# Moving operands of 512 columns read by turns from their two halves

## The chip, the core and the metric

The kernel runs on one core of a Trainium2 chip. A core has five engines that work beside each other and wait for each other through semaphores: TensorE (PE in the rows, with PEld for the loads of its stationary operand), VectorE (DVE), ScalarE (ACT), GpSimd (POOL) and SyncE (SP), which here issues nearly all DMAs. Matrix products are written by TensorE into eight PSUM banks of 128 partitions x 512 float32; VectorE and ScalarE read them there. Everything else lies in SBUF, 128 partitions wide. The metric is the device time of one execution in microseconds (us); lower is better.

## The reference

What has to be computed is an attention inside chunks of 64 tokens, followed by a gated feed-forward layer on all 4608 tokens, in float32:

```python
# q, k, v: (8, 8, 576, 64), chunks of 64 tokens
scores = scale * np.matmul(q_c, k_c.transpose(0, 1, 2, 4, 3))
scores = scores - np.max(scores, axis=-1, keepdims=True)
attn = np.exp(scores)
attn = attn / (np.sum(attn, axis=-1, keepdims=True) + 1e-09)
out = np.matmul(attn, v_c)
# x: the same numbers as (4608 tokens, 512)
g = x @ w_gate                       # 512 x 1536
silu = g * (1.0 / (1.0 + np.exp(-g)))
val = x @ w_val                      # 512 x 1536
return (silu * val @ w_out)          # 1536 x 512
```

## The kernel before, in words

**Tiling.** The 4608 tokens are nine blocks of 512. The 1536 inner features are twelve groups (`f`) of 128. A product of the feed-forward layer is a chain of matmuls into one PSUM bank, 128 features x 512 tokens. Each factor is kept as two parts of type float32r, an upper one (`hi`, `xh`, `hh`) and the rest (`lo`, `xl`, `hl`), and each product is the sum of three matmuls (lo times hi, hi times lo, hi times hi). The stationary operand is a 128x128 piece of weights (or, in `project`, of activations), loaded anew for each matmul; the moving operand has 512 columns of 4 bytes, side by side in SBUF.

**Stages.** In the opening (`opening`, a written list of steps) the scores, the softmax and the attention of blocks 0 and 1 are done, with the first matmuls of the layer (`some`, line 507) between them. For `f` 2 and 3 whole products follow (`gate`, `value`). From `f` 4 on (`first_seven`) blocks 0 and 1 are taken as a pair, and eight products of quarters are replaced by seven (`seventh`, line 919) whose results are combined by copies on ScalarE (lines 959, 967, 978) and additions on VectorE (`add`, line 923). Then block 2 is done with whole products (line 507), and blocks 3 to 8 in three pairs: twelve `gated_steps` with the seven products of line 919, each followed by some of the output product (`Left.project`, `quarter_of`, line 1283), and then `seven_products`, where the rest of the output product runs in units (`unit`, line 1283). Its results are taken by `snapshot` (ScalarE, line 1386) and `finish` (VectorE, line 1383), turned back by 32x32 transposes and stored. The last three units of the last pair are done for 384 tokens (line 1283) and then for the other 128 with 256 moving columns (`unit_by_tokens`, line 1369).

**Who reads a bank.** ScalarE: the silu of a gate (lines 539, 1005, 1440), the plain copies (959, 967, 978, 1413, 1415, 1417), `snapshot` (1386) and the evacuation of the output tokens of blocks 0 to 2 (line 587, which also swaps columns: `mixed`, `parted`). VectorE: the product with the value (`times`, line 546, where its input is a bank), `add` (923) and `finish` (1383). A bank is refilled when its reader is done; `ps1` is refilled three times in each step.

**Order.** PE, ACT and DVE are under a manual schedule throughout: each engine's instructions run in the order of the program. SP and POOL are scheduled freely after the start.

Other operands that the prediction compares with: line 696 (`B`) subtracts a maximum in PSUM with the moving operand `top[...].broadcast_to(...)`, 512 columns that are 8 numbers of 4 bytes, each read 64 times; lines 94 and 102 (`scale`, `below`) are reads by ScalarE whose neighbouring elements lie 8 bytes apart for `t<-raw`, and, through `order = parted, mixed`, 16 bytes apart for `wo<-raw` and `o_sb<-raw`; line 1574 and the last use of line 1383 (`back`) read a bank as `p (u s) -> p s u`, that is, by turns from two places 512 or 1024 bytes apart.

Of the kernel before, what the change touches and what calls it, by code (L numbers as in the profile page):

```python
# [14 lines left out]
ALU = mybir.AluOpType  # L15
# [18 lines left out]
def attn_then_gated_ffn(ctx: ExitStack, tc: tile.TileContext, qk, v, wgv, wo, out):  # L34
# [25 lines left out]
    def keep_warm_long(n):  # L60

        ps = ps_gv.tile([P, T, P], F32, name="unread", tag="ps_gv")
        for _ in range(n):
            nc.tensor.matmul(ps, ident, ident.rearrange("p (o k) -> p o k", o=1).broadcast_to([P, T, P]), start=True, stop=True)

# [437 lines left out]
    def some(ps, a, f, g, which, first=True, last=True):  # L503
        for k, i in which:
            w = (w_hi, w_lo, w_hi)[i][f][:, g, k]
            x = a.x[k // 2][i == 0][:, k % 2]
            nc.tensor.matmul(ps, w, x, start=first and (k, i) == which[0], stop=last and (k, i) == which[-1])  # L507
# [29 lines left out]
    def silu(pg):  # L537
        h = hp.tile([P, N], F32, name="h")
        nc.scalar.activation(h, pg, AF.Silu, scale=2.0 ** -8)
        return h  # L540
# [4 lines left out]
    def times(h, pv):  # L545
        nc.vector.scalar_tensor_tensor(out=h, in0=pv, scalar=2.0 ** -8, in1=h, op0=ALU.mult, op1=ALU.mult)  # L546

    def gated(a, f):
        h = gate(a, f)
        times(h, value(a, f))  # L550
        return h
# [10 lines left out]
    def project(parts, wo_f, which=range(T)):  # L562
# [6 lines left out]
        for t in which:  # L569
            ts, o = slice(t * P, (t + 1) * P), a.o[t]  # L570
            for at in (slice(0, DM // 2), slice(DM // 2, DM)) if (a.b, f) == (1, 2) or (a.b, f, t < 3) == (1, 3, True) else (slice(0, DM),):
                nc.tensor.matmul(o[:, at], hl[:, ts], woh[:, at], start=f == a.steps[0], stop=False)  # L572
            nc.tensor.matmul(o, hh[:, ts], wol, start=False, stop=False)  # L573
            nc.tensor.matmul(o, hh[:, ts], woh, start=False, stop=f == a.steps[1])  # L574
            if f == a.steps[1]:
# [11 lines left out]
                nc.scalar.activation(mixed(o_sb), parted(o), AF.Copy, scale=2.0 ** -8)  # L587
# [244 lines left out]
    for do in opening.split():  # L832
# [21 lines left out]
        elif do[0] == "Q":  # L854
            b, f = int(do[1]), int(do[2])
            times(rows_of[b, f], products[f"{'VD'[b]}{f}"].ps)
        else:
            b, i = int(do[1]), int(do[2])
            pairs = do[0] in "STCUL"
            getattr(couples[b, i // 2 if pairs else i], do[0])(i if pairs else int(do[3:] or 0))  # L860
# [10 lines left out]
    for f in range(2, SEVEN):  # L871
# [7 lines left out]
        times(h1, pv1)  # L879
# [9 lines left out]
        times(h0, pv0)  # L889
# [20 lines left out]
    times(h1, pv1)  # L910
# [3 lines left out]
    def seventh(ps, x, factors, i, first):  # L914
        which, q = FACTORS[i]
        w = [t.rearrange("p (i k m) -> p i k m", i=4, m=P)[:, q] for t in factors[which]]
        for k in range(NK // 2):
            for n, (u, v) in enumerate(((0, 1), (1, 0), (0, 0))):
                nc.tensor.matmul(ps, w[u][:, k], x[i][v][:, k], start=first and k == 0 and n == 0,  # L919
                                 stop=k == NK // 2 - 1 and n == 2, skip_group_check=True)  # L920

    def add(t, ps):
        nc.vector.tensor_tensor(out=t, in0=t, in1=ps, op=ALU.add)  # L923
# [8 lines left out]
    def first_seven(f, done, before):  # L932
# [26 lines left out]
        nc.scalar.copy(out=h, in_=ps1)  # L959
# [7 lines left out]
        nc.scalar.copy(out=v2, in_=ps2)  # L967
# [10 lines left out]
        nc.scalar.copy(out=v1, in_=ps1)  # L978
# [26 lines left out]
        nc.scalar.activation(h2, ps1, AF.Silu, scale=2.0 ** -8)  # L1005
# [273 lines left out]
    def quarter_of(to, hi, lo, w, u, first, at=slice(0, N), terms=range(3)):  # L1279
        w = w.rearrange("p j (u m) -> p j u m", u=2)  # L1280
        for n in terms:
            a, i = ((lo, 0), (hi, 1), (hi, 0))[n]
            nc.tensor.matmul(to, w[:, i, u], a[:, at], start=first and n == 0, stop=n == 2, skip_group_check=True)  # L1283

    class Seven(Pair):
# [96 lines left out]
        def finish(self, c, ps):  # L1382
            nc.vector.scalar_tensor_tensor(out=c, in0=ps, scalar=2.0 ** -8, in1=c, op0=ALU.mult, op1=ALU.add)

        def snapshot(self, c, ps):
            nc.scalar.activation(c, ps, AF.Copy, scale=2.0 ** -8)
# [13 lines left out]
    def gated_steps(pair, middle, mid, behind, bursts, nothing=lambda: None):  # L1400
        for f in range(NF):
# [11 lines left out]
            nc.scalar.copy(out=h, in_=ps1)  # L1413
            seventh(ps2, pair.x, loaded[f], 1, True)
            nc.scalar.copy(out=v2, in_=ps2)
            seventh(ps1, pair.x, loaded[f], 2, False)
            nc.scalar.copy(out=v1, in_=ps1)
# [22 lines left out]
            nc.scalar.activation(h2, ps1, AF.Silu, scale=2.0 ** -8)  # L1440
# [22 lines left out]
    def seven_products(pair, n):  # L1463
# [117 lines left out]
        pair.finish(back, ps.rearrange("p (u s) -> p s u", u=2))  # L1581
# [153 lines left out]
```

## Time and profile before

| | us |
|---|---|
| median of 3 runs (lowest, highest) | 865.46 (864.99, 865.77) |
| the profiled execution | 864.5 |
| its span, first to last instruction | 862.7 |
| PE busy in it | 853.7 (99%) |
| DVE busy | 652.7 (76%) |
| ACT busy | 424.5 (49%) |
| DMA, mean over the span | 252 GB/s |
| mean granted TensorE clock | 0.999 |

The profiled execution lies 1.0 us under the median, and 1.8 us of it lie outside its span. Read PE's 99% with care: a matmul's recorded duration holds the drain of the array, and the next one starts before it ends, so a row with one duration does not say how often a matmul can start. That is read from the starts of neighbouring rows.

### The profile page before, as it was taken

Reading aid. Unit: us, or ns where it says so; the run is one execution under the profiler, and the core shown is the slowest. Engines: PE = TensorE matmul, PEld = TensorE weight load, DVE = VectorE, ACT = ScalarE, POOL = GpSimd, SP = SyncE. Lnnn points to the kernel's source line nnn. Section 1 sums busy time; section 2 is a strip of 40 time slices with the busy share of each in tenths; the row PEclk is TensorE's granted clock in tenths of the full one; section 3 lists DMA queues with packets and bytes.
Section 4 is the critical chain, followed back from the end, with each engine's and each line's share of the span. In section 5 each row is a group of like instructions: output and inputs, shape, how many; then the busy total and the mean of one; then the engine's idle time right before and its main releaser. Section 6 shows DMA issues by size and latency. Waiting matters only on the chain.

```text
span 862.7 us, 14859 instructions
## 1 busy us (share of the span) xinstructions
PE 853.7 (99%) x5910; PEld 705.4 (82%) x5910; DVE 652.7 (76%) x944; ACT 424.5 (49%) x600; POOL 99.9 (12%) x94
## 2 busy tenths in 40 slices
PE   7999999999999999999999999999999999999998
PEld 5888888888888888888888888888888888888887
DVE  6988999777797673788897985887979943335785
ACT  4957788653524444536435635344346533333362
POOL 2100000000048743433200000000000000000000
PEclk9999999999999999999999999999999999999999
DMA  9967778899998785798976885766756965555562
GB/s 347 336 241 293 265 275 331 321 318 337 299 359 307 269 282 176 263 336 251 300 219 223 262 253 167 280 218 227 206 198 220 281 206 190 188 201 186 189 193 73
DMA packets 126948, 217.50 MB, mean 252 GB/s; under 512 B 56736, under 2 KB 88096, under 8 KB 116896
## 3 DMA queue, kind: packets, MB, share of 16 engines
q1 hardware_dynamic: 124560, 213.68, 72.9%
q10 hardware_dynamic: 2320, 2.88, 1.0%
q8 instruction: 46, 0.75, 0.4%
q14 instruction: 22, 0.18, 0.1%
HBM read 166.72 MB, written 49.81 MB: 251 GB/s over the span
## 4 chain that ended last, share of the span: by engine, by line
PE 97%; DMA 1%; ACT 0%; SPq 0%; issue 0%; DVE 0%; DVEq 0%
PE ps_a L919 28%; PE ps_gv L919 21%; PE ps_o L1283 14%; PE ps_gv L507 13%; PE ps_gv L1283 6%; PE ps_o L572 4%; PE ps_o L573 4%; PE ps_o L574 4%; PE ps_a L313 2%; PE ps_a L398 1%; DMA qk_t<-in_qk 1%; PE ps_a L497 1%; PE ps_a L1369 0%; PE ps_a L483 0%; ACT s_sb L700 0%; ACT pT L723 0%
## 5 line engine op out<-in xcount | busy, mean ns | idle before, releaser
L919 PE MATMUL ps_a<-x,factors 128*128 128x512 f32 x864 | 215.6, 390 | 0.0
L919 PEld LDWEIGHTS ps_a<-x,factors 128*128 128x128 f32 x864 | 161.9, 188 | 34.5 <-ACT s_sb L321 1.0
L919 PE MATMUL ps_gv<-x,factors 128*128 128x512 f32 x648 | 164.5, 389 | 0.0
L919 PEld LDWEIGHTS ps_gv<-x,factors 128*128 128x128 f32 x648 | 121.5, 188 | 25.4
L507 PE MATMUL ps_gv<-xh,w 128*128 128x512 f32 x320 | 97.3, 391 | 0.0
L385 DVE STREAM_TRANSPOSE turned<-s_sb 32x256 f32<-32x256 f32 x192 | 83.6, 436 | 2.7
L1283 PE MATMUL ps_o<-halves,sums 128*128 128x512 f32 (+1 forms) x324 | 72.8, 383 | 0.0
L507 PEld LDWEIGHTS ps_gv<-xh,w 128*128 128x128 f32 x320 | 59.9, 188 | 12.4
L1283 PEld LDWEIGHTS ps_o<-halves,sums 128*128 128x128 f32 x324 | 60.4, 188 | 11.3
L507 PE MATMUL ps_gv<-xl,w 128*128 128x512 f32 x160 | 60.7, 393 | 0.0
L546 DVE SCALAR_TENSOR_TENSOR rows<-v,rows 128x512 f32<-128x512 f32 x72 | 50.6, 703 | 13.2 <-ACT rows L1440 6.0
L923 DVE TENSOR_TENSOR rows<-rows,ps_gv 128x512 f32<-128x512 f32 x36 | 24.6, 685 | 44.5 <-PE ps_gv L919 43.8
L1429 ACT ACTIVATE rows<-rows 128x512 f32<-128x512 f32 x36 | 22.8, 633 | 71.6 <-DVE rows L923 71.6
L1283 PE MATMUL ps_o<-hh,left 128*128 128x512 f32 x216 | 57.7, 394 | 0.0
L1265 ACT CAST hh<-rows 128x512 fp32r<-128x512 f32 x36 | 22.4, 621 | 70.4 <-DVE rows L546 70.4
L572 PE MATMUL ps_o<-both,hh 128*128 128x512 f32 (+1 forms) x151 | 56.4, 381 | 0.0
L573 PE MATMUL ps_o<-both,hh 128*128 128x512 f32 x144 | 56.1, 390 | 0.0
L574 PE MATMUL ps_o<-both,hh 128*128 128x512 f32 x144 | 56.1, 390 | 0.0
L923 DVE TENSOR_TENSOR v<-v,ps_a 128x512 f32<-128x512 f32 x44 | 30.1, 685 | 28.9 <-PE ps_a L919 18.0
L1326 DVE TENSOR_TENSOR halves<-rows,halves 128x1024 fp32r<-128x1024 f32 x36 | 43.2, 1215 | 11.1 <-ACT halves L1322 11.0
L1283 PE MATMUL ps_gv<-halves,sums 128*128 128x512 f32 x216 | 50.4, 389 | 0.0
L1322 ACT CAST halves<-rows 128x1024 fp32r<-128x1024 f32 x36 | 37.2, 1053 | 21.5 <-DVE rows L1300 7.7
(171 smaller groups left out, 1367.0 us busy)
## 6 DMA issues: line engine op xcount, KB each, us to landing
factors<-t SPq DMA_DIRECT2D x36, 1024.0 KB, 6.9
factors<-w SPq DMA_DIRECT2D x36, 512.0 KB, 4.1
w<-w SPq DMA_DIRECT2D x16, 1024.0 KB, 7.8
sums<-s SPq DMA_DIRECT2D x15, 1024.0 KB, 4.9
qk_t<-in_qk SPq DMA_DIRECT2D x26, 512.0 KB, 7.8
t<-th SPq DMA_DIRECT2D x24, 512.0 KB, 3.9
raw<-in_wgv SPq DMA_DIRECT2D x11, 1024.0 KB, 7.7
both<-o SPq DMA_DIRECT2D x22, 512.0 KB, 6.4
```

The lines of the kernel that those rows point to most:

```text
L385: nc.vector.transpose(out=self.turned[to:to + 32, p:p + 2, j, :, 32 * (i % 2):32 * (i % 2) + 32], in_=src[32 * i:32 * i + 32, :, o // 2, 3 ...
L507: nc.tensor.matmul(ps, w, x, start=first and (k, i) == which[0], stop=last and (k, i) == which[-1])
L546: nc.vector.scalar_tensor_tensor(out=h, in0=pv, scalar=2.0 ** -8, in1=h, op0=ALU.mult, op1=ALU.mult)
L572: nc.tensor.matmul(o[:, at], hl[:, ts], woh[:, at], start=f == a.steps[0], stop=False)
L573: nc.tensor.matmul(o, hh[:, ts], wol, start=False, stop=False)
L574: nc.tensor.matmul(o, hh[:, ts], woh, start=False, stop=f == a.steps[1])
L919: nc.tensor.matmul(ps, w[u][:, k], x[i][v][:, k], start=first and k == 0 and n == 0, stop=k == NK // 2 - 1 and n == 2, skip_group_check=True)
L923: nc.vector.tensor_tensor(out=t, in0=t, in1=ps, op=ALU.add)
L1283: nc.tensor.matmul(to, w[:, i, u], a[:, at], start=first and n == 0, stop=n == 2, skip_group_check=True)
L1322: nc.scalar.copy(out=t[:, 0], in_=src)
L1326: nc.vector.tensor_tensor(out=lo, in0=src, in1=hi.bitcast(F32), op=ALU.subtract)
L1429: nc.scalar.activation(h, h, AF.Silu, scale=2.0 ** -8)
```

## The change

Two things are done, always together.

1. The moving operand of the matmuls with 512 columns (and of those with 384, and of the pieces of 256 at line 572) is read through `by_turns`: column 0, column 256, column 1, column 257, and so on. The first index steps by 4 bytes, the inner one jumps by half of the operand (1024 bytes). The columns of the result stand in the bank in that order, without gaps.
2. Whatever reads such a bank reads it through `put_back`: first every second column from 0 on, then every second from 1 on (a step of 8 bytes), and so writes the columns to SBUF in their old order. At line 587 the bank's new order and the swap of columns cancel in part: the bank is read with steps and the output is written side by side.

Not touched: the matmuls of the attention (64x64), the transposes, line 696, and line 1369.

```diff
+    def by_turns(x):
+        return x.rearrange("p (a b) -> p b a", a=2)
+
+    def put_back(ps):
+        return ps.rearrange("p (b a) -> p a b", a=2)
+
+    def in_halves(x):
+        return x.rearrange("p (a b) -> p a b", a=2)
...
-            nc.tensor.matmul(ps, w, x, start=first and (k, i) == which[0], stop=last and (k, i) == which[-1])
+            nc.tensor.matmul(ps, w, by_turns(x), start=first and (k, i) == which[0], stop=last and (k, i) == which[-1])
...
-        nc.scalar.activation(h, pg, AF.Silu, scale=2.0 ** -8)
+        nc.scalar.activation(in_halves(h), put_back(pg), AF.Silu, scale=2.0 ** -8)
...
-    def times(h, pv):
-        nc.vector.scalar_tensor_tensor(out=h, in0=pv, scalar=2.0 ** -8, in1=h, op0=ALU.mult, op1=ALU.mult)
+    def times(h, v):
+        nc.vector.scalar_tensor_tensor(out=h, in0=v, scalar=2.0 ** -8, in1=h, op0=ALU.mult, op1=ALU.mult)
+
+    def times_bank(h, pv):
+        times(in_halves(h), put_back(pv))
...
-                nc.tensor.matmul(o[:, at], hl[:, ts], woh[:, at], start=f == a.steps[0], stop=False)
-            nc.tensor.matmul(o, hh[:, ts], wol, start=False, stop=False)
-            nc.tensor.matmul(o, hh[:, ts], woh, start=False, stop=f == a.steps[1])
+                nc.tensor.matmul(o[:, at], hl[:, ts], by_turns(woh)[:, at.start // 2:at.stop // 2], start=f == a.steps[0], stop=False)
+            nc.tensor.matmul(o, hh[:, ts], by_turns(wol), start=False, stop=False)
+            nc.tensor.matmul(o, hh[:, ts], by_turns(woh), start=False, stop=f == a.steps[1])
...
-                nc.scalar.activation(mixed(o_sb), parted(o), AF.Copy, scale=2.0 ** -8)
+                nc.scalar.activation(o_sb.rearrange("p (h s u) -> p h s u", h=2, u=2), o.rearrange("p (u s h) -> p h s u", h=2, u=2), AF.Copy, scale=2.0 ** -8)
...
-                nc.tensor.matmul(ps, w[u][:, k], x[i][v][:, k], start=first and k == 0 and n == 0,
+                nc.tensor.matmul(ps, w[u][:, k], by_turns(x[i][v][:, k]), start=first and k == 0 and n == 0,
...
     def add(t, ps):
-        nc.vector.tensor_tensor(out=t, in0=t, in1=ps, op=ALU.add)
+        t = in_halves(t)
+        nc.vector.tensor_tensor(out=t, in0=t, in1=put_back(ps), op=ALU.add)
...
-            nc.tensor.matmul(to, w[:, i, u], a[:, at], start=first and n == 0, stop=n == 2, skip_group_check=True)
+            nc.tensor.matmul(to, w[:, i, u], by_turns(a[:, at]), start=first and n == 0, stop=n == 2, skip_group_check=True)
...
         def finish(self, c, ps):
-            nc.vector.scalar_tensor_tensor(out=c, in0=ps, scalar=2.0 ** -8, in1=c, op0=ALU.mult, op1=ALU.add)
+            c = in_halves(c)
+            nc.vector.scalar_tensor_tensor(out=c, in0=put_back(ps), scalar=2.0 ** -8, in1=c, op0=ALU.mult, op1=ALU.add)
 
         def snapshot(self, c, ps):
-            nc.scalar.activation(c, ps, AF.Copy, scale=2.0 ** -8)
+            nc.scalar.activation(in_halves(c), put_back(ps), AF.Copy, scale=2.0 ** -8)
```

The plain copies out of a bank (lines 959, 967, 978, 1413, 1415, 1417) and the silus of lines 1005 and 1440 change as `silu` does; the last `finish` (`back`) is written out as it was, since line 1369 is untouched.

No instruction is added, removed or moved: on every engine the same instructions stand in the same order, on the same buffers. What differs beside the access patterns is some waits: 97 matmuls in place of 27 also wait for an earlier matmul, the nearest of them 15 matmuls back, and 32 additions on VectorE lose a wait for ScalarE.

## Rows read from the trace of the kernel before

**Rows 1.** The page: busy time (share of the span) and instructions; the chain by engine.
```profile
PE 853.7 (99%) x5910; PEld 705.4 (82%) x5910; DVE 652.7 (76%) x944; ACT 424.5 (49%) x600; POOL 99.9 (12%) x94
...
PE 97%; DMA 1%; ACT 0%; SPq 0%; issue 0%; DVE 0%; DVEq 0%
```

**Rows 2.** Whole span, lines 919, 1283, 507, 572, 573 (574 alike): PE (count), PEld.
```profile
0.00:863.00 863.00, 432.22 (x1848) 346.24 (x1848) 1.00 0.74 252
...
0.00:863.00 863.00, 178.51 (x756) 140.82 (x756) 1.00 0.74 252
...
0.00:863.00 863.00, 113.17 (x480) 89.50 (x480) 1.00 0.74 252
...
0.00:863.00 863.00, 56.36 (x151) 28.35 (x151) 1.00 0.74 252
...
0.00:863.00 863.00, 56.09 (x144) 27.04 (x144) 1.00 0.74 252
```

**Rows 3.** Timeline of PE: first start, us to the last end, line, tile, shape, count.
```profile
9.27 0.81 PE L696 MATMUL ps_a<-tops,minus 128*128 128x512 f32 x3
...
619.26 2.88 PE L919 MATMUL ps_a<-x,factors 128*128 128x512 f32 x12
621.98 1.52 PE L919 MATMUL ps_gv<-x,factors 128*128 128x512 f32 x6
...
854.88 1.55 PE L1283 MATMUL ps_o<-halves,sums 128*128 128x384 f32 x8
...
856.61 2.31 PE L1369 MATMUL ps_a<-sums,halves 128*128 128x256 f32 x18
```

**Rows 4.** Lines 696, 919, 1283, 1369: duration in ns, least/median/most.
```profile
L696 PEld LDWEIGHTS ps_a<-tops,minus x16: 186/189/192, 8.9 to 18.8; 128*128 128x128 f32 x16
L696 PE MATMUL ps_a<-tops,minus x16: 379/379/483, 8.9 to 19.0; 128*128 128x512 f32 x16
...
L919 PEld LDWEIGHTS ps_gv<-x,factors x648: 186/188/188, 323.7 to 812.9; 128*128 128x128 f32 x162
...
L919 PEldq EVENT_SEMAPHORE  x31: 51/51/51, 318.5 to 769.9; - x31
...
L1283 PE MATMUL ps_o<-halves,sums x42: 333/334/423, 848.7 to 856.4; 128*128 128x384 f32 x36, 128*128 128x512 f32 x6
...
L1369 PE MATMUL ps_a<-sums,halves x18: 278/283/283, 856.6 to 858.6; 128*128 128x256 f32 x18
```

**Rows 5.** Groups on ACT and DVE by shape: busy us, mean ns, idle before.
```profile
L94 ACT ACTIVATE wo<-raw 128x512 f32<-128x512 f32 x12 | 13.5, 1128 | 0.1
...
L1386 ACT ACTIVATE c<-ps_o 128x512 f32<-128x512 f32 x18 | 10.1, 592 | 6.0 <-PE ps_o L1283 4.7 <-DMA factors<-w 1.0
...
L94 ACT ACTIVATE t<-raw 128x512 f32<-128x512 f32 x2 | 1.3, 674 | 3.0 <-DMA raw<-in_wgv 3.0
...
L1574 ACT COPY back<-pt 128x256 f32<-128x256 f32 x1 | 0.4, 372 | 2.8 <-PE pt L1573 2.8
...
L1383 DVE SCALAR_TENSOR_TENSOR c<-ps_o,c 128x384 f32<-128x384 f32 x2 | 1.1, 557 | 2.6 <-PE ps_o L1283 2.6
L1383 DVE SCALAR_TENSOR_TENSOR back<-ps_a,back 128x256 f32<-128x256 f32 x1 | 0.4, 425 | 1.0 <-PE ps_a L1369 1.0
```

**Rows 6.** By stage: us, busy PE PEld DVE ACT POOL (count), clock, DMA, GB/s.
```profile
84.00:165.00 81.00, 81.00 (x356) 66.38 (x355) 74.27 (x108) 64.97 (x87) 0.00 (x0) 1.00 0.77 299
165.00:215.00 50.00, 50.00 (x469) 41.75 (x468) 33.95 (x61) 21.50 (x34) 0.00 (x0) 1.00 0.95 331
...
458.00:500.00 42.00, 42.00 (x187) 34.77 (x186) 40.05 (x42) 25.69 (x31) 0.00 (x0) 1.00 0.77 250
...
640.00:682.00 42.00, 42.00 (x187) 34.80 (x186) 40.94 (x43) 24.84 (x30) 0.00 (x0) 1.00 0.77 242
```

**Rows 7.** Waits of weight loads, 84 to 165 us: total us, times, longest.
```profile
PEld ps_a L919 <- DVE v L923: 0.4, 1, 0.4
PEld ps_a L919 <- ACT v L978: 0.4, 1, 0.4
```

## What the change does to the time: a prediction

> **What bounds the kernel now.** First the page: TensorE is busy for 853.7 of 862.7 us and makes 97% of the chain that ended last [rows 1]. So what a matmul costs decides, and other engines count only where they make TensorE wait. Second, which matmuls: the counts by line [rows 2] are 1848 + 756 + 480 + 151 + 144 + 144 (line 574 as line 573). Of these, 36 of line 1283 have 384 columns [rows 4] and 14 of line 572 have 256, which leaves 3473 with 512. Third, how often one can start, from the starts in the timeline [rows 3]. Line 919 has 12 matmuls between 619.26 and 621.98 us: 2.72 us / 12 = 226.7 ns. With the granted clock at 0.999 of 2.4 GHz, 512 columns alone would be 213.3 ns. Line 1283 with 384 columns: the eighth starts 1.55 us less one duration of 334 ns [rows 4] after the first, so 1.216 / 7 = 173.7 ns, against 160.0 for the columns. Line 1369 with 256: (2.31 - 0.283) / 17 = 119.2 ns, against 106.7. The surplus is 13.4, 13.7 and 12.5 ns: the same for each matmul, however many columns it has. Fourth, one line is different: 696, also 512 columns, with a weight load of the same length (189 against 188 ns, [rows 4]), starts every (0.81 - 0.379) / 2 = 215.5 ns [rows 3, 4]. Its moving operand is 8 numbers read over and over. Array, weight load and write to PSUM are the same as elsewhere, so 226.7 - 215.5 = 11.2 ns of each matmul belong to the read of a moving operand that runs through memory. As this does not grow with the columns, I take it for something that happens once per matmul; the weight load (128 columns each time) that is read from the same memory meanwhile is my candidate. That is an inference, and no row shows two reads collide.
>
> **The change part by part.** *The moving read.* What a read by turns from two places costs TensorE stands in no row. The bound below: the whole 11.2 ns goes, as in line 696, since then a column that is held up in one half need not hold up the next, which comes from the other. The bound above: reads that leave a 16-byte stretch of SBUF with each element. ScalarE has such a read at line 94: 128x512 from `raw` with a step of 16 bytes takes 1128 ns, with a step of 8 bytes 674 [rows 5], so 454 ns more for 512 elements. Here a read returns to the same stretch with the next column but one, which that row doesn't do. I take the lower bound, since line 696 is the same engine and the same instruction and line 94 is neither, and keep the upper as the first rival.
>
> The Trainium skill speaks against the change here: "Advanced Engine Details and Errata", section "Memory Cachelines", has SBUF lines of 16 bytes, wants two hits on a line for full speed and puts a penalty on a different line with each access. The step of 16 bytes in line 94 agrees with it (1128 against 674 ns). By that rule the sum below would change its sign; whether TensorE keeps two lines at hand no row shows.
>
> The sum: 3473 matmuls with 512 columns and 36 with 384, 3509 x 11.2 ns = 39.3 us, if TensorE never waits more than now. The 14 pieces of 256 I leave at nothing.
>
> *What is late next.* Three places cannot follow. From 84 to 165 us (`first_seven`) TensorE has 356 matmuls, 4.0 us of the sum; weight loads there already wait for the copy at line 978 and the addition at line 923 (0.4 us each, [rows 7]), with VectorE busy for 74.27 and ScalarE for 64.97 of 81 us [rows 6]. `ps1` comes free only when a reader in the middle of their queues is done, and that does not get faster: I keep 1.0 of the 4.0 us. In the two stages of `seven_products` (458 to 500 and 640 to 682 us) TensorE has 187 matmuls, 2.1 us each, and VectorE is busy for 40.05 and 40.94 of 42 us [rows 6]; 42 - 2.1 = 39.9 is less than that. I keep half, 2.1 of 4.2. From 165 to 215 us the DMA engines have a share of 0.95 [rows 6]; I take off 1 us. The opening's first matmuls of line 507, before the softmax chain ends, give nothing: under 0.2 us. Together 39.3 - 3.0 - 2.1 - 1.0 - 0.2 = 33 us. The whole 39.3 stays if all slack suffices; 26.7 if these losses, 6.3 us together, are twice as large.
>
> *The readers of the banks.* They now step by 8 bytes in PSUM. The nearest rows read a bank by turns from two places: ScalarE at line 1574 takes 372 ns for 256 elements, against 592 for 512 side by side at line 1386, that is 0.86 ns for each of the 256 more; VectorE's `back` at line 1383 takes 425 for 256, against 557 for 384 side by side [rows 5], 1.03 ns for each. With a penalty on steps the shorter reads would lie high, and they do not. So I cost the readers at nothing; a gain has no reason, as the elements stay as many; above, 454 ns for each read as in line 94, which is the second rival. They run beside TensorE, except at the places just named.
>
> *The waits.* 70 more matmuls also wait for an earlier matmul, 15 or more before it, so over 3 us back at 215 ns each. Behind them the next matmuls would be held up, and the readers of the banks after them, but what they wait for is long done. What stays is a semaphore instruction on TensorE's queue: the 31 at line 919 take 51 ns each [rows 4], beside running matmuls. Nothing.
>
> Sum against the profiled execution: 864.5 - 33 = 831.5 us. The median of the runs lies 1.0 above that execution: **832.5 us**, told as 833.
>
> **The rivals.** *First, slower: each column is a new line.* If TensorE pays for each column what ScalarE pays at line 94, a matmul takes 226.7 + 454 = 681 ns and the kernel 865.5 + 3473 x 0.454 = 2442 us. If a column costs as much as one element of a plain read does on ScalarE, 0.86 ns as above, it is 440 ns, 213 more, and 1605 us. It decides from any start-to-start time over 226.7 ns, since nothing hides a matmul. For it: line 94, the only row with a line per element in SBUF. Against it: contiguous reads here pay a fixed amount, not one per line, and a read by turns stays in each line for four of its columns.
>
> *Second, slower: the put-back costs.* TensorE gains nothing and each reader of a bank takes 454 ns more. From 84 to 165 us there are seven steps of `first_seven` with three additions of line 923 each: VectorE 74.27 + 21 x 0.454 = 83.8 of 81 us. In each of the two product stages it has at most 8 such reads (line 1383): 43.7 and 44.6 of 42. That is 2.8 + 1.7 + 2.6 = 7 us, 872; and if in each of the 44 steps of seven products one bank is late by those 454 ns, 20 more, 892. It decides once a reader takes longer than the slack that TensorE leaves it. Against it: lines 1574 and 1383 [rows 5].
>
> *Third: the change doesn't do what it says.* The 11.2 ns belong to every read that runs through memory, whatever its order: 865.5 us. For it: all contiguous operands pay it alike. Against it: so fixed an amount looks like a meeting with the weight load. The Trainium skill's "SBUF — State Buffer", section "Who interferes with whom", gives TensorE two independent read ports, one for the moving operand and one for weights; by that my candidate is wrong and this rival is the outcome, though the rule leaves line 696's 215.5 ns unexplained.
>
> **How the numbers follow.** Forecast, faster: 0.66. First rival 0.18, second 0.09, third 0.07. The forecast's own range: with the whole 39.3 us kept 826, and 823 if the surplus over the bare columns goes as well in part; with 26.7 kept 839; with half of the 11.2 ns gone 849. The range that I give is 823 to 895: it takes in the third rival and the second to its 892, 0.82 in all less the tails, and leaves out the first, for whose prices no bound near the others exists. A difference under 0.2%, 1.7 us, is about what a measurement of this kernel cannot tell from no change. Faster 0.66, within it 0.07, slower 0.27 (first and second rival).
>
> **What would show it.** Right: neighbouring matmuls of line 919 and 1283 start about 216 ns apart, their recorded duration falls from 389 to about 379 ns as in line 696, and waits of TensorE for `v`, `h` and `halves` grow to some 6 us in the three stages. The readers keep their durations (592 ns at line 1386). Wrong: starts 227 ns apart (third rival) or some 430 to 680 (first), or copies of line 1413 and additions of line 923 that take a microsecond and more (second). If the starts fall to 216 and the time falls by less than 20 us, my slack was wrong and not the read.

## The result, and the profile after

The changed kernel takes 844.92 us (median of 4 runs, 843.64 to 845.34), the kernel before 865.23 beside it: a ratio of 0.9763, 95% interval 0.9746 to 0.9780. It is faster, by 20 us. Forecast were 833 us and a range of 823 to 895.

Lines have moved: 919 is now 933, 1283 is 1298, 1383 is 1399, 1386 is 1402, 923 is 938, 94 and 102 are 105 and 113, 959 and 978 are 974 and 993, 1326 is 1341, 1373 is 1388. First the page of the profiled execution (span 843.3 us), as in [rows 1]:

```profile
PE 822.9 (98%) x5910; PEld 707.5 (84%) x5910; DVE 656.0 (78%) x944; ACT 438.1 (52%) x600; POOL 100.7 (12%) x94
...
PE 68%; DVE 16%; DMA 6%; ACT 5%; issue 3%; SPq 1%; DVEq 0%; ACTq 0%
```

TensorE was 97% of the chain and is 68% now: VectorE, loads and ScalarE stand between its pieces. Then the starts, as in [rows 3], and the durations and readers, as in [rows 4, 5] (timeline of PE; groups by shape):

```profile
611.72 1.46 PE L933 MATMUL ps_gv<-x,factors 128*128 128x512 f32 x6
613.01 1.46 PE L933 MATMUL ps_a<-x,factors 128*128 128x512 f32 x6
614.31 1.46 PE L933 MATMUL ps_gv<-x,factors 128*128 128x512 f32 x6
```
```profile
L933 PE MATMUL ps_a<-x,factors 128*128 128x512 f32 x864 | 206.8, 380 | 2.7 <-ACT halves L1337 1.5
L1402 ACT ACTIVATE c<-ps_o 128x512 f32<-128x512 f32 x18 | 10.2, 594 | 4.4 <-PE ps_o L1298 4.2
L938 DVE TENSOR_TENSOR v<-v,ps_gv 128x512 f32<-128x512 f32 x44 | 30.1, 684 | 10.2 <-PE ps_gv L933 10.2
```

Twelve matmuls start in 614.31 - 611.72 = 2.59 us, 216 ns each, where it was 226.7. The readers of the banks, which now step by 8 bytes, take what they took (594 ns against 592). But reads of SBUF that the change doesn't touch became slower, if they step (ScalarE's lines 105 and 113 unpack words with steps of 16 and 8 bytes; VectorE's line 1388 turns a block):

```profile
L113 ACT ACTIVATE o_sb<-raw 128x512 int32<-128x512 uint32 x12 | 18.7, 1555 | 0.0
L105 ACT ACTIVATE wo<-raw 128x512 f32<-128x512 f32 x12 | 18.4, 1530 | 0.5 <-DMA raw<-in_wo 0.5
L105 ACT ACTIVATE t<-raw 128x512 f32<-128x512 f32 x2 | 1.3, 662 | 2.6 <-DMA raw<-in_wgv 2.6
...
L1388 DVE STREAM_TRANSPOSE turned<-c 128x512 f32<-128x512 f32 x22 | 19.0, 862 | 0.8
```

The copies of `wo` rose from 1128 [rows 5] to 1530 ns, the transposes from 714 to 862; the two early pieces of `t` (662, before 674), which run before the first matmul by turns, did not change. What TensorE waited for (weight loads, as in [rows 7]), in `first_seven` (86 to 167 us) and in the second stage of `seven_products` (627.5 to 669.5 us; the first stage has the same two rows with 1.3 us each), and these stages as in [rows 6]:

```profile
PEld ps_a L933 <- ACT h L974: 3.4, 4, 1.1
PEld ps_a L933 <- DVE v L938: 2.5, 4, 0.7
PEld ps_a L933 <- ACT v L993: 1.7, 6, 0.7
```
```profile
PEld ps_o L1298 <- DVE halves L1341: 1.5, 2, 0.9
PEld ps_o L1298 <- PE ps_o L1298: 1.3, 1, 1.3
```
```profile
86.00:167.00 81.00, 77.96 (x350) 64.44 (x349) 73.20 (x106) 71.40 (x84) 0.00 (x0) 1.00 0.74 289
167.00:217.00 50.00, 50.00 (x508) 43.44 (x510) 34.87 (x62) 22.49 (x35) 0.00 (x0) 1.00 0.98 344
449.00:491.00 42.00, 40.57 (x186) 34.71 (x185) 38.60 (x40) 26.12 (x33) 0.00 (x0) 1.00 0.78 253
627.50:669.50 42.00, 40.42 (x184) 34.27 (x184) 39.70 (x41) 25.60 (x31) 0.00 (x0) 1.00 0.72 234
```

The row in which line 1298 waits for itself is VectorE's too: that wait is for a semaphore of TensorE and one of VectorE, and in all eight traces that read by turns there it ends 44 to 46 ns after VectorE's subtraction of line 1341 (here at 490.47 and 490.43 us). Where TensorE never paused before, it now pauses, and ScalarE is busy for 71.40 us in the first stage where it was 64.97.

To see where time was won, the table takes the same matmuls in each kernel: the time from the start of the one that began a stretch before to the start of the one that ended it. "Possible" is the count of changed matmuls with 384 or 512 columns in the stretch times 11.2 ns. "Late", "16 bytes", "mixed" and "GpSimd" are experiments 4, 6, 9 and 10 below, "before + GpSimd" is 12. Each column is one profiled execution.

| stretch before, us | possible | before | after | late | 16 bytes | mixed | GpSimd | before + GpSimd |
|---|---|---|---|---|---|---|---|---|
| 0-46 | 0.94 | 44.81 | 46.86 | 44.90 | 44.14 | 45.64 | 45.91 | 45.83 |
| 46-168 | 5.99 | 121.84 | 122.19 | 121.82 | 119.62 | 119.60 | 122.08 | 121.82 |
| 168-345 | 7.94 | 177.12 | 169.81 | 170.48 | 171.17 | 169.92 | 171.11 | 177.12 |
| 345-441 | 4.40 | 96.03 | 93.16 | 93.77 | 93.30 | 92.85 | 92.66 | 96.03 |
| 441-458 | 0.72 | 16.87 | 17.12 | 17.13 | 19.07 | 17.86 | 17.13 | 16.86 |
| 458-500 | 2.08 | 42.16 | 42.25 | 42.25 | 42.06 | 42.25 | 43.37 | 43.23 |
| 500-620 | 5.57 | 119.98 | 114.64 | 114.64 | 114.64 | 114.64 | 114.66 | 120.03 |
| 620-640 | 0.87 | 20.03 | 21.44 | 21.14 | 22.47 | 22.25 | 21.40 | 20.04 |
| 640-682 | 2.07 | 41.93 | 42.40 | 42.40 | 41.85 | 42.03 | 43.16 | 42.99 |
| 682-end | 8.71 | 176.51 | 168.03 | 168.02 | 168.02 | 168.02 | 168.03 | 176.51 |

In all 39.3 us were possible, 19.4 came, 19.9 are lost: 3.0 in the opening, 6.3 from 46 to 168, 1.5 from 345 to 441, 1.0, 2.2, 2.3 and 2.5 in the four stretches around the stages of seven products, 1.1 in the rest. From 500 to 620 and from 682 on nearly all arrives (13.8 of 14.3). The opening differs by some 1 us between executions without any change there (44.81 and 45.83 in the two columns of before).

### The profile page after: what moved, and what is told of

It reads as the page before. It is cut to its first block, busy times and chain, and to the rows that moved or that the text cites. A ratio compares the mean times of both kernels' runs of the same rounds, so it can differ in the third digit from the quotient of the medians.

```text
span 843.3 us, 14878 instructions
## 1 busy us (share of the span) xinstructions
PE 822.9 (98%) x5910; PEld 707.5 (84%) x5910; DVE 656.0 (78%) x944; ACT 438.1 (52%) x600; POOL 100.7 (12%) x94
## 4 chain that ended last, share of the span: by engine, by line
PE 68%; DVE 16%; DMA 6%; ACT 5%; issue 3%; SPq 1%; DVEq 0%; ACTq 0%
PE ps_a L933 21%; PE ps_gv L933 15%; PE ps_o L1298 10%; PE ps_gv L518 9%; DMA raw<-in_wgv 4%; PE ps_o L586 3%; PE ps_o L587 3%; PE ps_o L588 3%; DVE halves L1341 2%; PE ps_gv L1298 2%; DVE turned L396 2%; PE ps_a L324 2%; DMA w<-w 2%; DVE rows L1315 1%; PE ps_a L409 1%
## 5 line engine op out<-in xcount | busy, mean ns | idle before, releaser
L933 PE MATMUL ps_a<-x,factors 128*128 128x512 f32 x864 | 206.8, 380 | 2.7 <-ACT halves L1337 1.5
L933 PE MATMUL ps_gv<-x,factors 128*128 128x512 f32 x648 | 157.7, 379 | 0.0
L518 PE MATMUL ps_gv<-xh,w 128*128 128x512 f32 x320 | 94.0, 380 | 0.2 <-DVE w L157 0.2
L1298 PE MATMUL ps_o<-halves,sums 128*128 128x512 f32 (+1 forms) x324 | 70.5, 375 | 3.0 <-PE ps_o L1298 1.8
L1298 PE MATMUL ps_o<-hh,left 128*128 128x512 f32 x216 | 55.3, 383 | 0.0
L587 PE MATMUL ps_o<-both,hh 128*128 128x512 f32 x144 | 54.6, 379 | 0.0
L588 PE MATMUL ps_o<-both,hh 128*128 128x512 f32 x144 | 54.6, 379 | 0.0
L1298 PE MATMUL ps_gv<-halves,sums 128*128 128x512 f32 x216 | 48.1, 379 | 0.0
```

The lines of the kernel that those rows point to most:

```text
L518: nc.tensor.matmul(ps, w, by_turns(x), start=first and (k, i) == which[0], stop=last and (k, i) == which[-1])
L587: nc.tensor.matmul(o, hh[:, ts], by_turns(wol), start=False, stop=False)
L588: nc.tensor.matmul(o, hh[:, ts], by_turns(woh), start=False, stop=f == a.steps[1])
L933: nc.tensor.matmul(ps, w[u][:, k], by_turns(x[i][v][:, k]), start=first and k == 0 and n == 0, stop=k == NK // 2 - 1 and n == 2, skip_grou ...
L1298: nc.tensor.matmul(to, w[:, i, u], by_turns(a[:, at]), start=first and n == 0, stop=n == 2, skip_group_check=True)
```

## The experiments

**1. The read by itself.** Bursts of 16 and 28 float32r matmuls whose moving operand of 512 columns is read in different orders, also with fewer weight columns, and beside copies of ScalarE and work of VectorE.

```
"four": x.rearrange("p (a b) -> p b a", a=4)        # four places, 512 bytes apart
"two", "step": every second, every fourth number    # steps of 8 and 16 bytes
"pairs": two columns here, two there                "held": 8 numbers over and over
"half", "quarter": side by side, 64 and 32 columns of weights
```

> Nothing of the reference is computed: bursts of 16 and 28 float32r matmuls over data in SBUF. Theory A (the surplus of 11 ns comes from the moving read meeting the weight load's read in the memory): side by side 226.7 ns, held columns 215.5, by turns 215.7; with 64 and 32 columns of weights the surplus of side by side falls to about a half and a quarter (221, 218). Theory B (the surplus is the moving read's own): 226.7 with 64 and 32 columns of weights as well. Theory A for the slower ScalarE (its reads that leave a 16-byte stretch with each element meet a read by turns): beside turns the copy with a 16-byte step takes about 1500 ns, beside side-by-side matmuls about 1100; with a step of 8 bytes about 750 against 670; side by side 590 to 620 in both. Rival: the slowing in the kernel came from elsewhere (DMA, VectorE); then all copies take the same beside either form.

Timeline of PE: start, us to the last end, count; then ScalarE's groups (each three copies: side by side, steps of 8 and of 16 bytes):

```profile
6.32 15.88 PE L79 MATMUL side<-columns,weights 128*128 128x512 f32 x56 [6.32 <-ACT columns L48]
22.25 3.72 PE L79 MATMUL turns<-columns,weights 128*128 128x512 f32 x16
26.03 4.78 PE L79 MATMUL four<-columns,weights 128*128 128x512 f32 x16
30.86 7.47 PE L79 MATMUL two<-columns,weights 128*128 128x512 f32 x16
38.39 7.62 PE L79 MATMUL step<-columns,weights 128*128 128x512 f32 x16
46.07 5.68 PE L79 MATMUL pairs<-columns,weights 128*128 128x512 f32 x16
...
59.42 3.72 PE L79 MATMUL held<-columns,weights 128*128 128x512 f32 x16
63.20 3.91 PE L79 MATMUL half<-columns,weights 128*64 128x512 f32 x16
67.17 3.89 PE L79 MATMUL quarter<-columns,weights 128*32 128x512 f32 x16
```
```profile
L99 ACT COPY turns<-source 128x512 f32<-128x512 f32 x3 | 2.9, 1039 | 0.0
...
L99 ACT COPY side<-source 128x512 f32<-128x512 f32 x3 | 2.2, 793 | 0.0
L99 ACT COPY two<-source 128x512 f32<-128x512 f32 x3 | 2.2, 787 | 0.0
```

Median start to start: side by side 227 ns, by turns 216, one held operand 216, four places 283, pairs 340, steps of 8 and 16 bytes 451 and 461. With 64 and 32 columns of weights, whose loads take 135 and 108 ns in place of 188, a read side by side still takes 231 and 232. So the surplus does not come from meeting the weight load; it is the read's own, and two places by turns are a case apart: four places already cost 67 ns. The three copies beside turns took 621, 891 and 1605 ns one by one, beside a read side by side 623, 649 and 1107, and beside the other four forms at most 673 and 1146 in the last two. What slows ScalarE is not that TensorE leaves a stretch at each column, which "step" does too; and four places, 512 bytes apart at 283 ns, slow nothing (654 and 1119 ns).

**2 and 3. The two halves of the change.** One kernel reads by turns and takes the banks side by side; the other reads side by side and steps through the banks.

```
 2:  def put_back(ps): return ps.rearrange("p (a b) -> p a b", a=2)
 3:  def by_turns(x):  return x.rearrange("p (b a) -> p b a", a=2)
```

> The moving operands are read by turns, the banks are read side by side, so the columns of the result stand in a wrong order. Theory (all of the change, gain and loss, is in TensorE's read): 845 us as with the whole change, lines 94 and 102 at 1500 to 1560 ns. Rival (the put-back readers slow ScalarE's strided reads or delay TensorE): lines 94 and 102 at 1130, and some 832 to 838 us.

> The moving operands are read side by side as before, the banks are read with steps of 8 bytes, so the columns of the result stand in a wrong order. Theory: 865 us, readers of banks at 0.59 (ScalarE) and 0.68 us (VectorE), lines 94 and 102 at 1130 to 1150 ns. Rival: 867 to 872 us and lines 94 and 102 slower.

```profile
L105 ACT ACTIVATE wo<-raw 128x512 f32<-128x512 f32 x12 | 18.4, 1531 | 0.2 <-DMA raw<-in_wo 0.2
```
```profile
L105 ACT ACTIVATE wo<-raw 128x512 f32<-128x512 f32 x12 | 13.5, 1126 | 0.3 <-DMA raw<-in_wo 0.3
```

Turns alone (first row): 844.77 us, ratio 0.9765 (0.9746 to 0.9783), as the whole change, with the slow copies. Putting back alone (second row): 866.35 us, 1.0013 (1.0004 to 1.0023), 1.1 us slower and at most 2.0, copies as before. Gain and harm both lie in TensorE's read; the readers of the banks are all but free.

**4 and 8. Turns only late, turns only early**, parted at the end of `first_seven`, some 171 us.

```
+    by = {"turns": False}         # 8: True
     _, h2 = first_seven(NF - 1, quarters, None)
+    by["turns"] = True            # 8: False
```

> Everything up to the end of first_seven (blocks 0 and 1, about 171 us) is as before, from block 2 on it is as with the change. Theory (the loss in the first 171 us is ScalarE's lines 94 and 102, slowed by the read by turns): these lines back at 1130 to 1150 ns, the first 171 us as before the change, so 2.2 us less than the whole change: 842.7 us. Rival (the two parts are not independent, the late part loses again what the early part keeps): 844 to 846 us.

> Turns of 1024 bytes as in the change until the end of the first seven-product stage at about 171 us, the order of before from there on: the complement of the kernel with late turns. At 171 us the changed kernel was 2.2 us late on the kernel before. Theory A, the loss up to there is real and is not made good: about 865.4 + 2 = 867, between 866 and 869, with the copies of the output weights at 1530 ns and starts of 216 ns up to 171 us and 227 after. Theory B, what is late there is caught up in later waits: 864.5 to 866.

Late turns: 843.97 us, ratio 0.9752 (0.9731 to 0.9774). Early turns: 867.14 us, 1.0018 (1.0009 to 1.0027). Up to 168 us 619 matmuls became shorter by 6.9 us together, and the program is slower for it: that is the harm on its own. Taking it away gave 1 us of 845, within the spread of the runs: of the 2.3 us that "late" was ahead at 168 us (0-46 and 46-168 of the table), it gave 1.3 back by 441.

**5. How far apart the two places lie.** The same bursts with groups in which the places are 8, 16, 64 and 256 bytes apart, halves 1024 apart, and halves moved to 1040.

```
def within(b): return lambda x: x.rearrange("p (g a b) -> p g b a", a=2, b=b)   # b = 2, 4, 16, 64
far = const.tile([P, 2, 260], F32R, name="apart")                               # 1040 bytes
```

> Nothing of the reference is computed here: the kernel holds only bursts of 28 float32r matmuls of 512 columns with other work beside them. The two places that TensorE reads by turns lie 8, 16, 64, 256, 1024 or 1040 bytes apart. Beside each form ScalarE copies 128x512 numbers with a step of 4, 8 and 16 bytes, and VectorE makes a transpose and two sums, one with a step of 16 bytes in one input. In the run of forms the reads in halves (1024 bytes apart) took 216 ns and the stepped copies beside them 891 and 1605 ns, where beside a read side by side they took 649 and 1107; the transpose took 872 and 702, the stepped sum 1532 and 1054. Theory A, the other engines are slowed because TensorE leaves one stretch of memory for another at every column: at 16 bytes' distance it mostly stays in the same stretch, so starts come 216 ns apart there as before while the stepped copies stay near 650 and 1110 ns, the transpose near 700 and the stepped sum near 1060; from some distance on, 64 bytes or more, they rise to about 890, 1600, 870 and 1530. Theory B, what slows them is that TensorE reads without the pauses that the 227 ns of a read side by side contain: then every form with starts 216 ns apart, however near its places are, shows about 890, 1600, 870 and 1530 ns. Theory C, the slowing comes from two places in the same bank, that is from a distance that is a multiple of some power of two: then 1040 bytes would leave the copies near 650 and 1110 ns and 1024 would not.

Start to start: 227 ns at 8 bytes, 216 at 16, 64, 256, 1024 and 1040. VectorE's groups beside them (the number in a name is the distance, "turns" is 1024 and "apart" 1040 bytes; "sumstep" reads one input with a step of 16 bytes, "back" is a transpose):

```profile
L106 DVE TENSOR_TENSOR turnssumstep<-source 128x512 f32<-128x512 f32 x1 | 1.5, 1519 | 0.0
L106 DVE TENSOR_TENSOR by256sumstep<-source 128x512 f32<-128x512 f32 x1 | 1.5, 1517 | 0.0
...
L106 DVE TENSOR_TENSOR apartsumstep<-source 128x512 f32<-128x512 f32 x1 | 1.1, 1096 | 0.0
...
L106 DVE TENSOR_TENSOR by16sumstep<-source 128x512 f32<-128x512 f32 x1 | 1.1, 1057 | 0.0
L106 DVE TENSOR_TENSOR sidesumstep<-source 128x512 f32<-128x512 f32 x1 | 1.1, 1052 | 0.0
...
L101 DVE STREAM_TRANSPOSE turnsback<-source 128x512 f32<-128x512 f32 x1 | 0.9, 870 | 0.0
L101 DVE STREAM_TRANSPOSE by256back<-source 128x512 f32<-128x512 f32 x1 | 0.9, 852 | 0.0
...
L101 DVE STREAM_TRANSPOSE apartback<-source 128x512 f32<-128x512 f32 x1 | 0.7, 705 | 0.0
```

ScalarE's copy with a step of 16 bytes took 1561 and 1605 ns beside 256 and 1024, 1092 to 1131 beside 8, 16, 64 and 1040. Theories A and B fall (64 is free, and so are 16 and 1040 with full speed); C stands as far as it was tried: the others' stepped reads are slowed where the two places lie 256 or 1024 bytes apart, and 16 bytes more than 1024 free them. Why is not shown, and other distances were not tried.

**6 and 7. The whole kernel with 16 and with 64 bytes.** VectorE's scalar_tensor_tensor has at most two steps besides the partition in all these traces, ScalarE's activation three; a bank whose order needs more is read in two instructions here.

```
-        return x.rearrange("p (a b) -> p b a", a=2)
+        return x.rearrange("p (g a b) -> p g b a", a=2, b=4)      # 7: b=16
-        times(in_halves(h), put_back(pv))
+        for i in range(2):
+            times(in_halves(h)[:, :, i], put_back(pv)[:, :, i])
```

> The whole kernel, with the two places that TensorE reads by turns 16 bytes apart instead of 1024 (groups of 8 columns, read 0, 4, 1, 5, 2, 6, 3, 7); the readers of the banks put that order back, in two instructions where VectorE's scalar_tensor_tensor and ScalarE's copy to the output take no more than two steps. Theory A, the loss of the changed kernel (some 19 of 38 us of shorter matmuls) comes largely from ScalarE's and VectorE's stepped reads, slowed because both places lie at a multiple of 256 bytes: starts stay at 216 ns, the copies of the output weights fall from 1530 to about 1130 ns, the turned products of VectorE from 862 to about 715, the gain at 171 us rises from -2.2 to between +1 and +5, and the time falls from 844.9 to between 834 and 842. Theory B, the loss is only TensorE being fast enough to wait for results that come no later than before: the copies fall as well, but the time stays at 843 to 847. Theory C, the extra split of the banks' readers (two instructions of 256 columns for one of 512 at some 50 places, about 0.1 us each) and a third step in the others' addresses cost more than they save: 847 to 853.

> As the kernel before it, with the two places 64 bytes apart (groups of 32 columns). In the run of distances this was as free as 16 bytes: starts 216 ns, transposes 702, stepped sums 1074 for 1057. Theory A: within 1 us of the kernel with 16 bytes, 834 to 842; Theory B: 843 to 847; if the inner runs of 4 columns cost the banks' readers something at 16 bytes, runs of 16 columns cost less, and this kernel is faster than the other by over 1 us.

With 16 bytes: 845.76 us (842.98 to 849.33), ratio 0.9779 (0.9752 to 0.9806); with 64: 845.93, 0.9775 (0.9759 to 0.9792). The slowing is gone while starts stay at 216 ns: copies of `wo` take 1134 ns, and VectorE's transposes with 16 bytes what they took before:

```profile
L1393 DVE STREAM_TRANSPOSE turned<-c 128x512 f32<-128x512 f32 x22 | 15.7, 713 | 0.8
```

And the stretch from 46 to 168 us takes 119.62 instead of 122.19 us (119.65 with 64 bytes), so 2.6 us of the lost 6.3 were this. But the time is the same: theory A is right for that stretch, theory B for the whole. The split has a price: two halves of a sum with a bank take 0.80 us where the whole took 0.67. What was won is lost at 262 to 300, 441 to 458 and 620 to 640 us, by 1.4, 1.9 and 1.0 us.

**9. 16 bytes early, 1024 late**, to tell whether the split readers take that back.

```
+    B, by = 4, {"groups": True}
     _, h2 = first_seven(NF - 1, quarters, None)
+    by["groups"] = False
```

> Places 16 bytes apart until the end of the first seven-product stage (some 171 us), 1024 bytes from there on, with one instruction for each reader of a bank there. The kernel with 16 bytes throughout got the early stretch back (168 us of the program took 165.3 there, 171.1 in the changed kernel) but lost about 1.4, 1.9 and 1.1 us at the three later places (262 to 300, 441 to 458 and 620 to 640 us), which are laid to its split readers. Theory A (that price is the split readers'): the three later stretches go back to 36.6, 17.1 and 21.4 us, the early one stays at 165 to 166, and the time is 839 to 842 us. Theory B (those gaps come from the earlier start of the rest, whatever the readers): they stay, and the time is 844 to 847.

843.93 us (841.78 to 847.70), ratio 0.9759 (0.9735 to 0.9782); the profiled execution has 840.5 us of span. 46 to 168 us stay at 119.60, 262 to 300 go back to 36.64, 441 to 458 to 17.86, but 620 to 640 take 22.25. Half an answer: experiments 2 and 10, whose readers are not split, have 37.81 and 37.98 in the second stretch, so these places move by 1 to 2 us without them.

At two of them the traces point to something that no experiment was made for. TensorE (first rows: experiment 6) stops with no releaser that the profile shows, there in the middle of 128 like matmuls; the last row is a DMA queue of the changed kernel's page (packets, MB, share), of the kind "instruction":

```profile
615.86 2.08 PE L411 MATMUL ps_a<-turned,v_t 64*64 64x64 f32 x120
620.54 0.34 PE L411 MATMUL ps_a<-turned,v_t 64*64 64x64 f32 x8 [2.60 <-issue]
...
q8 instruction: 47, 0.77, 0.4%
```

A packet of 16 KB of that queue landed at 619.17 us, 1.4 us before TensorE went on. All eight traces that read by turns there have such a pause, of 1.2 to 2.6 us, and in all of them it ends 1.3 to 1.7 us after a packet has landed, wherever in the chain it falls; the kernels that read side by side there have none. The pauses at 443 us in experiments 6 and 7 (1.9 and 1.8 us) are of the same kind. With 47 packets for TensorE's 11820 matmuls and loads, one for some 250, this looks like TensorE waiting for its own program to be loaded, now that it comes there sooner. It fits every trace, but no run moved a packet, so it is not shown.

In the median experiment 9 is 1 us below the changed kernel and not to be told from it; no version beat both kernels by more than the runs differ.

**10, 11 and 12. Less work for VectorE in the seven products.** There TensorE now waits (start, us, what ended the idle time) where it ran through before:

```profile
480.79 2.86 PE L1298 MATMUL ps_o<-halves,sums 128*128 128x512 f32 x12
484.19 5.45 PE L1298 MATMUL ps_o<-halves,sums 128*128 128x512 f32 x24 [0.55 <-DVE halves L1341]
490.53 8.01 PE L1298 MATMUL ps_o<-halves,sums 128*128 128x512 f32 x36 [0.88 <-PE ps_o L1298]
```

```
-            nc.vector.tensor_tensor(out=lo, in0=self.from_[i], ...)
+            (nc.gpsimd if i < 3 else nc.vector).tensor_tensor(out=lo, in0=self.from_[i], ...)
```

> The changed kernel, with three of the seven subtractions that make the low parts of the next pair's rows (x_lower, 128x1024, 1.22 us each on VectorE) on GpSimd in each of the two middle stages of seven products, where VectorE works without a pause and TensorE now waits twice, 0.9 and 1.2 us, for VectorE's low halves. Theory A, the lost time of those stages (42.25 and 42.40 us for 186 and 185 matmuls, of which the shorter matmuls alone would make 40.1 and 39.9) is VectorE's work ahead in its queue: 3.4 us less of it there lets both stages fall to 40.0 to 40.8, and the time falls by 3 to 4 us, to 840.5 to 842. Theory B, the wait is for something else (the copies of ScalarE, a load): the stages keep 42 us and the time stays at 844 to 846. If GpSimd's subtractions (about 3 us each by the 1.58 us of its 128x512) come too late for the products that read them, the time rises over 846.

> Both edits together: 16 bytes early and 1024 late, three subtractions a stage on GpSimd. They act in different stretches of the program, so their gains should add: by theory A of each 836 to 838.5 us; if one of the two is void, 840 to 842.

> The kernel before with the same three subtractions a stage on GpSimd. There the two stages are TensorE's without a gap (42.16 us for 186 matmuls of 226.7 ns), so theory A of the edit on GpSimd, that VectorE became the bound there only with the shorter matmuls, expects no gain: 864 to 866 us, ratio 0.999 to 1.001. A gain of 3 us or more here would mean that the edit helps by another way and tells nothing of the lost time.

Measured: 846.26 us, ratio 0.9783 (0.9768 to 0.9798); both edits 846.34, 0.9777 (0.9764 to 0.9791); before with the edit 868.12, 1.0029 (1.0017 to 1.0040). None of the forecast gains came, and the kernel before lost 2.5 us. The stages became longer, 43.37 and 43.16 us. GpSimd, VectorE and TensorE in the first of them:

```profile
477.09 3.34 POOL L1353 TENSOR_TENSOR x<-sum,x 128x1024 fp32r<-128x1024 f32 x1 [4.04 <-ACT x L1348]
483.81 2.39 POOL L1353 TENSOR_TENSOR x<-s_sb,x 128x1024 fp32r<-128x1024 f32 x1 [3.38 <-ACT x L1348]
```
```profile
478.95 2.56 DVE L1341 TENSOR_TENSOR halves<-rows,halves 128x1024 fp32r<-128x1024 f32 x1 [0.76 <-ACT halves L1337]
...
482.57 1.21 DVE L1341 TENSOR_TENSOR halves<-rows,halves 128x1024 fp32r<-128x1024 f32 x1
484.70 2.57 DVE L1341 TENSOR_TENSOR halves<-rows,halves 128x1024 fp32r<-128x1024 f32 x1 [0.92 <-ACT halves L1337]
```
```profile
481.57 5.45 PE L1298 MATMUL ps_o<-halves,sums 128*128 128x512 f32 x24 [0.95 <-DVE halves L1341]
491.38 8.01 PE L1298 MATMUL ps_o<-halves,sums 128*128 128x512 f32 x36 [1.19 <-issue]
```

The edit did not do what it was for: beside GpSimd's subtraction one of VectorE takes 2.57 us and not 1.21. Of the 3.7 us that it got back in a stage VectorE paid 2.7 for two such meetings, and before both it now waits for ScalarE, 0.76 and 0.92 us. What a free VectorE would give stays untested. But the edit in the kernel before tells the margin there:

```profile
499.85 8.46 PE L1283 MATMUL ps_o<-halves,sums 128*128 128x512 f32 x36 [0.74 <-DVE halves L1326]
```

The low halves that TensorE needs at 499.85 come from a subtraction that began at 498.61 and not at 496.42; 1.0 us of that is the whole program's lag (line 1383 at 479.60 and 478.61). 1.2 us of delay on VectorE cost TensorE 0.74 there and 1.07 in the stage (43.23 against 42.16), so the margin was 0.1 to 0.5 us by this estimate. The trace of the kernel before has it directly (VectorE, then the weight load that needs its result):

```profile
496.42 1.19 DVE L1326 TENSOR_TENSOR halves<-rows,halves 128x1024 fp32r<-128x1024 f32 x1
...
497.70 0.19 PEld L1283 LDWEIGHTS ps_o<-halves,sums 128*128 128x128 f32 x1
```

The subtraction ended at 497.60 us, 0.10 us before the load began. By this point shorter matmuls put TensorE 2 us ahead.

## Why the prediction was right in its sign and 12 us off

That the time lies in the range says little: 823 to 895 us held the third rival, no change, as well. The starts are the test of the mechanism, and the 20 us of the sum; by the sum's own bounds 26.7 to 39.3 us should have been kept.

- **The read: right.** 11.2 ns of each matmul, because line 696's starts of 215.5 ns are what the other lines now show (216); durations 379 to 380; the 39.3 us of the sum are what the table has as possible.
- **The candidate behind it: wrong.** Fewer weight columns leave the surplus (experiment 1). It came where neighbouring columns lie less than 16 bytes apart: 227 ns side by side and with 8 bytes between the places, 216 with 16. One number read again (line 696) does not pay it. Why it does not grow with the columns, no run shows.
- **The first rival: wrong for this read.** Its price was of the right size for a step of 16 bytes (461 ns where it said 440 at the low end; that is chance, for 440 came from a plain read on another engine), but two places by turns are not that read. By the rule of the Trainium skill quoted there ("Advanced Engine Details and Errata", section "Memory Cachelines"), a new line with each access is slow and two hits on a line are enough: the runs agree for the step of 16 bytes (461 ns) and four places (283), and not for two places (216), nor for the step of 8 bytes, two hits on a line, which takes 451.
- **The readers of the banks: right**, 594 for 592 ns, and at most 2 us for all of them (experiment 3).
- **The added waits: right.** Stand-alone semaphore instructions of line 933 rose from 31 to 74, the median still 51 ns; the one long wait that bears such a mark, line 1298's for itself, was for VectorE (see the result).
- **What is late next: the step that failed.** 6.3 us were taken off for it, 19.9 are lost. Its sign, waits of some 6 us in the three stages, came (3.0, 1.4 and 1.6 us idle), but a matmul's duration of 379 ns hides up to 163 ns of each wait; the same matmuls, start to start, lost 10.2 us there. By its own places:
  - 84 to 165 us, 3.0 taken off: 5.5 lost (from 84 to 168 us 83.99 rose to 85.32, with 4.1 possible). With 16 bytes that stretch takes 83.49, 3.6 lost. So the slack was judged about right, and the rest is the contention: the step kept ScalarE's 64.97 us as they were, and they became 71.40.
  - the two stages of `seven_products`, 2.1 taken off: 4.7 lost, more than all that was possible there. Half the gain was kept with VectorE busy for 40.05 and 40.94 of 42 us; but the share said too little: the next input was done only 0.1 us before its use (experiment 12). What the slower transposes add is open: eight in each stage, 0.15 us longer each, are 1.2 us of VectorE's time; experiment 6, where they are short again (42.06 and 41.85 us for 42.25 and 42.40), has eight split sums there that cost about as much.
  - 165 to 215 us, 1.0 taken off: 0.2 lost. The share of the DMA engines rose to 0.98, and TensorE did not wait.
  - the opening to 84 us, 0.2 taken off: 3.9 lost. 0.75 of it is contention (46 to 84 us: 36.87, with 16 bytes 36.12). Up to 46 us single executions differ by over 1 us, but all traces together tell a part: with reads side by side these matmuls take 44.81 to 45.83 us (four traces), with places 16 or 64 bytes apart 44.14 to 45.73 (four), with 1024 45.91 to 47.59 (four). So some 1.6 us, by the means, go with the distance there too; the rest stays open.
  - not seen at all: 441 to 458 and 620 to 640 us, 3.3 lost, and 1.5 from 345 to 441. At 441 and 616 us TensorE waits for `v` of line 938, whose addition stands behind eight transposes and an operation of line 1315 in VectorE's queue (3.59 and 1.23 us). The largest pause, 1.5 us at 622, the profile lays to a copy of ScalarE, in experiments 6 and 9 to nothing ("issue", 2.7 and 2.5 us); an instruction packet landed 1.65 us before its end, as told at experiment 9: open.

The prediction said what it would mean if starts fell to 216 and the time by less than 20 us. The time fell by 20.3, just past that mark: the read was right, the slack was too generous.

## What to carry to other kernels

When the busiest engine has hardly a pause, price a faster instruction twice: the sum of what it saves, and for each input that it takes from another engine how long before its use it is done. Here VectorE's busy time left 2 us of 42 and the trace before showed 0.1 us at the hand-over; the hand-over decided. A new address pattern on one engine is also an edit to every engine that reads the same memory meanwhile; look there for instructions that nobody changed and that take longer. Of the distances tried for two places read by turns, 16, 64 and 1040 bytes left the other engines alone and 256 and 1024 did not; in the whole kernel 16 and 64 mended the copies, and the time stayed the same.

## What the runs showed of the hardware beyond that

- TensorE at 216 ns a matmul can slow ScalarE and VectorE: with places 256 or 1024 bytes apart their reads of SBUF in steps take 1561 to 1605 ns for 1102 (16 bytes, ScalarE) and 1517 to 1519 for 1052 (VectorE), transposes 852 to 870 for 705; contiguous reads don't change (621 and 622). The Trainium skill ("SBUF — State Buffer", section "Who interferes with whom") lets only VectorE and GpSimd contend; here the measurement decides against it.
- For TensorE, 512 columns cost 216 ns by turns between two places of 16 or more bytes' distance, 227 side by side, 283 from four places, 340 in pairs by turns, 451 and 461 in steps of 8 and 16 bytes.
- A subtraction of 128x1024 on GpSimd makes one on VectorE beside it take 2.57 us and not 1.21; there that same section of the Trainium skill and the trace agree.
